# Loading the short cache in 32 KB runs, eight heads to a slot, and moving the softmax weights between the V matmuls, in a one-core decode attention kernel

## The chip, the cores and the metric

The kernel runs on one core of one Trainium2 chip. The metric is the device time of one execution in microseconds (us). Executions of one kernel agree here within about 1% (the kernel before: 248.27 to 251.29 us over 7 runs). Times quoted are medians over an experiment's runs, with the lowest and highest in brackets.

Names: PE is the matmul engine (TensorE), DVE the vector engine, ACT the scalar engine, SP the engine whose queue issues the bulk loads. SBUF is the memory that the loads fill and that `slots` and `kt` lie in, addressed here as 128 partitions; PSUM is the memory that the matmuls of this kernel write.

## The reference, cut to what matters

Two attention decode steps, A and B, of one token each, independent of each other. Both have 32 query heads on 16 key/value heads, head size 128, and a cache of 8192 positions in bf16. A looks only at the last 2048 positions, B at all of them.

```python
D, Hq, Hkv, Sk, Dh = 576, 32, 16, 8192, 128
def attend(x, k_cache, v_cache, wq, wo, W):          # A: W = 2048, B: W = 8192
    q = (x @ wq) as [32 heads, 128]
    k, v = k_cache[:, :, Sk - W:, :], v_cache[:, :, Sk - W:, :]   # each serves 2 query heads
    p = softmax(q @ k.T * Dh ** -0.5)
    return (p @ v) as [1, 4096] @ wo                 # wo: [4096, 576]
out = concatenate([A, B], axis=-1)                   # [1, 1, 1152]
```

A's K and V are 16 heads x 2048 x 128 x 2 bytes = 8.39 MB each, 16.8 MB together. B's are 67.1 MB. The four weight matrices add 18.9 MB, which gives the 102.8 MB that the profile counts.

## The kernel before, where the change touches it

The cache passes through four slots of SBUF, two for K and two for V, each of 128 partitions x 32 KB = 4 MB. There are five groups: group 0 is all of A, groups 1 to 4 are four heads of B each, two heads to a slot. In a slot of B, partition 2p+e holds 128 consecutive positions (32 KB) of head e. For A a head has only 2048 positions, so before the change a slot was filled by four loads of two heads each, and a partition held four runs of 32 positions (8 KB), one of each load:

```python
def load_kv(arrs, g, s, off, res, name):
    dst = slots[:, off:off + SLOT]                       # SLOT = 16384 bf16 = 32 KB
    def go(sp):
        if g:                                            # B
            i = 4 * (g - 1) + 2 * s
            return sp.dma_start(dst, arrs[1][0, i:i + 2, :, :].rearrange("e (p t) d -> p e (t d)", t=128))
        for m in range(4):                               # A: four loads of 1 MB
            i = 4 * m + 2 * s
            src = arrs[0][0, i:i + 2, SK - W_A:, :].rearrange("e (p t) d -> p e (t d)", t=32)
            ins = sp.dma_start(dst[:, m * UNIT:(m + 1) * UNIT], src)     # UNIT = 4096
            ...                                          # all four count on one semaphore
```

Each group then runs the same loop body: K is transposed on PE, 32 blocks of 128x128 at a time, and copied from PSUM to `kt` by ACT and DVE in turn (128x1024 each); scores; one exp; P transposed; V:

```python
def k_transpose(g, u, place):
    for q in range(4):
        ...                                              # 8 transposes into PSUM bank q
        dst = kt[:, u % NKT, q * 1024:(q + 1) * 1024]    # a plain copy, ACT for even q, DVE for odd q
def v_slot(g, s, place):                                 # 32 weights each
    for tt in range(8):
        for j in range(4):
            pe.matmul(opsum[32*j:32*j+32, s*512:(s+1)*512], lhsT=ptm[:, tt*128+32*j : ... +32],
                      rhs=v[:, :, (8*j+tt)*128 : ... +128], start=(tt == 0), stop=(tt == 7))
def v_keep(g):                                           # keep the wanted head's part, sum over the 8 parts
    diag = opsum * maskV                                 # DVE, 128x1024
    acc[:, g, :] = sum(diag)                             # DVE
```

After the last group come the final softmax weights, the output projection (`ktps`, 128 matmuls of 144 columns for A, 128 for B) and the store. The loads of `wo` go into slots that are already free:

```python
for g in range(NG):                                      # NG = 5
    ...                                                  # loads, k_transpose, k_scores, softmax_exp
    softmax_transpose(g, 18)
    if g == NG - 1:
        weights(g)                                       # before V
        combine(0, ...)
    v_slot(g, 0, 20); v_slot(g, 1, 21); v_keep(g)
wo_loads = [(0, 0, 32, ...), (1, 0, 24, ...), (1, 24, 5, ...), (1, 29, 2, ...), (1, 31, 1, ...)]  # (A or B, first column, columns)
combine(1)
...                                                      # wo_part per load, then finish_out
```

## Time and profile before

| what | value |
|---|---|
| time | 248.95 us before the change was tried; 249.53 (248.82 to 250.72, 4 runs) beside it |
| bulk load queue | 102.77 MB, 97.0% of the 16 DMA engines' time |
| PE busy | 67% of the span; DVE and ACT 35% each |
| rate of the loads while A's cache streams (26 to 62 us) | 421 GB/s |
| rate while B's streams (64 to 218 us) | 432 GB/s |

From the page of the kernel before: the DMA engines' busy share in tenths and the rate in 40 slices of the span, the bulk queue's line, and the start of the chain of work that ended last.

```profile
...
DMA  9998999999999999999999999999999999999980
GB/s 350 410 463 372 421 423 421 420 421 420 446 449 438 433 423 427 422 422 443 434 433 438 433 427 427 427 433 433 433 438 443 422 427 433 422 454 411 433 334 9
...
q1 hardware_dynamic: 5632, 102.77, 97.0%
...
PE 8%; DVE 3%; issue 1%; ACT 0%
PE opsum L540 3%; PE ktps L627 2%; PE misc L612 1%; DVE acc L384 1%; DVE diag L548 0%; DVE accs L599 0%; DVE ptm L527 0%; PE misc L518 0%; PE misc L589 0%; PE misc L577 0%; PE misc L559 0%; PE misc L578 0%; PE misc L590 0%; PE misc L560 0%;
...
```

The load stream is busy nearly everywhere and its rate hardly changes, so whatever makes the bytes arrive sooner shortens the kernel. The page's chain ends in the tail's compute. The busy table by stage of the same kernel gives the two rates that the prediction uses; the last three columns are the clock granted to PE, the DMA engines' busy share, and GB/s:

```profile
...
core 0: us, PE busy (x) PEld busy (x) DVE busy (x) ACT busy (x) POOL busy (x), PEclk, DMA share, GB/s
26.00:62.00 36.00, 27.27 (x400) 19.73 (x393) 14.20 (x24) 17.52 (x19) 0.63 (x4) 0.89 1.01 421
64.00:218.00 154.00, 112.48 (x1568) 81.25 (x1568) 63.04 (x88) 67.48 (x72) 1.88 (x12) 0.83 1.00 432
...
```

The timeline of the tail: start, duration, engine, line and operation, count, and in brackets how long the engine was idle before and what ended it.

```profile
...
237.37 3.43 PE L627 MATMUL ktps<-slots,opj 128*32 128x144 bf16 x102
...
242.01 2.18 PE L627 MATMUL ktps<-slots,opj 128*32 128x144 bf16 x127 [1.21 <-issue]
...
245.84 0.54 PE L627 MATMUL ktps<-slots,opj 128*32 128x144 bf16 x21 [1.65 <-issue]
...
246.41 0.31 DVE L633 CAST outsb<-ktps 128x144 bf16<-128x144 f32 x1 [3.55 <-PE ktps L627]
```

The output projection stops twice, 1.21 us and 1.65 us, waiting for nothing that the profile shows ("issue"). The instruction queue moved a packet of 16 KB from 239.6 to 240.7 us and one from 243.2 to 244.4 us; the stops begin at 240.8 and 244.2 us. What PE waits for in them is not shown.

### The profile page before, as it was taken

The page shows a single profiled execution, that of the slowest core. Times are in us where ns is not written, and L with a number is a line of the kernel's source. Part 1 is how long each engine was busy: PE and PEld are TensorE (multiplying, and loading weights), DVE is VectorE, ACT ScalarE, POOL GpSimd, SP SyncE. Part 2 cuts the span into 40 slices and gives each one's busy share as a digit, 9 for nine tenths or more (in the row PEclk, how much of TensorE's full clock was granted, in tenths as well). Part 3 has the DMA queues.
Part 4 walks back from the last instruction along what each step waited for, and adds up shares of the span by engine and source line. Part 5 has one row for each costly group of instructions (what it writes and reads, how often), then busy time and mean ns, then how long its engine had stood idle before and what let it go on. Part 6 is the DMA issues. An engine that isn't in the chain of part 4 may idle for free. (4 is left out here: it accounts for less than half of the span.)

```text
span 248.4 us, 5439 instructions
## 1 busy us (share of the span) xinstructions
PE 165.4 (67%) x2428; PEld 117.5 (47%) x2428; DVE 87.3 (35%) x140; ACT 87.3 (35%) x95; POOL 10.7 (4%) x48
## 2 busy tenths in 40 slices
PE   0026839992818997625999463999470999559374
PEld 0012428770408875315876223887230987335173
DVE  0001044552142555141565231656222356330500
ACT  2000027782004776102786101778100678500000
POOL 7400000000000000000000000000000000000000
PEclk9999797998595999795999775999775699955759
DMA  9998999999999999999999999999999999999980
GB/s 350 410 463 372 421 423 421 420 421 420 446 449 438 433 423 427 422 422 443 434 433 438 433 427 427 427 433 433 433 438 443 422 427 433 422 454 411 433 334 9
DMA packets 5929, 102.89 MB, mean 414 GB/s; under 512 B 928, under 2 KB 1056, under 8 KB 1312
## 3 DMA queue, kind: packets, MB, share of 16 engines
q1 hardware_dynamic: 5632, 102.77, 97.0%
q8 instruction: 6, 0.10, 0.2%
q10 hardware_dynamic: 288, 0.00, 0.1%
q14 instruction: 3, 0.02, 0.0%
HBM read 102.76 MB, written 0.00 MB: 414 GB/s over the span
## 5 line engine op out<-in xcount | busy, mean ns | idle before, releaser
L472 ACT ACTIVATE kt<-ktps 128x1024 bf16<-128x1024 bf16 x80 | 78.4, 1021 | 88.4 <-PE ktps L466 88.2
L466 PE MATMUL ktps<-ident,slots 128*128 128x128 bf16 x1280 | 87.7, 234 | 32.2 <-PEq L214 30.0
L466 PEld LDWEIGHTS ktps<-ident,slots 128*128 128x128 bf16 x1280 | 81.7, 106 | 47.6 <-issue 47.6
L475 DVE COPY kt<-ktps 128x1024 bf16<-128x1024 bf16 x80 | 55.3, 691 | 68.8 <-PE ktps L466 68.8
L540 PE MATMUL opsum<-slots,ptm 128*32 128x512 bf16 x320 | 28.7, 537 | 4.2 <-PEq L214 4.2
L487 PE MATMUL sacc<-kt,qst 128*32 128x512 bf16 x320 | 25.4, 392 | 1.9 <-PEq L214 1.9
L425 PE MATMUL opsum<-slots,xpad 128*32 128x512 bf16 x144 | 11.2, 482 | 19.0 <-DVE xpad L413 19.0
L540 PEld LDWEIGHTS opsum<-slots,ptm 128*32 128x32 bf16 x320 | 11.6, 129 | 20.0 <-issue 17.9
L425 PEld LDWEIGHTS opsum<-slots,xpad 128*32 128x32 bf16 x144 | 5.1, 117 | 24.3 <-issue 22.6
L548 DVE TENSOR_TENSOR diag<-opsum,maskV 128x1024 f32<-128x1024 f32 x5 | 6.1, 1225 | 29.3 <-PE opsum L540 29.3
L518 PE MATMUL misc<-ident,psb 128*128 128x128 bf16 x40 | 3.9, 257 | 11.6 <-PEq L214 11.6
L431 ACT ACTIVATE qrow<-opsum 128x512 bf16<-128x512 f32 x2 | 1.2, 597 | 27.3 <-PE opsum L425 27.3
L456 POOL COPY qst<-qcol 128x8 bf16<-128x8 bf16 x20 | 3.1, 191 | 162.3 <-PE sacc L487 148.2
L508 ACT ACTIVATE psb<-sacc,stat 128x1024 bf16<-128x1024 f32 x5 | 5.6, 1114 | 11.9 <-DVE stat L502 11.9
L518 PEld LDWEIGHTS misc<-ident,psb 128*128 128x128 bf16 x40 | 2.9, 114 | 14.0 <-issue 14.0
L384 DVE TENSOR_REDUCE acc<-diag 128x128 f32<-128x1024 f32 x5 | 9.4, 1871 | 0.2
L487 PEld LDWEIGHTS sacc<-kt,qst 128*32 128x32 bf16 x320 | 5.0, 94 | 7.9 <-issue 4.3
L527 DVE TENSOR_SCALAR ptm<-misc,par 128x512 bf16<-128x512 bf16 x10 | 4.4, 481 | 11.1 <-PE misc L518 11.1
L627 PE MATMUL ktps<-slots,opj 128*32 128x144 bf16 x256 | 6.4, 268 | 2.9 <-issue 2.9
L627 PEld LDWEIGHTS ktps<-slots,opj 128*32 128x32 bf16 x256 | 5.7, 118 | 3.3 <-issue 3.3
L413 DVE TENSOR_SCALAR xpad<-xtwo,par 128x5 bf16<-128x5 bf16 x4 | 0.7, 232 | 13.8 <-DMA xtwo<-in_A_x_dram 12.4
L433 DVE CAST qrow<-opsum 128x512 bf16<-128x512 f32 x2 | 1.4, 692 | 11.6 <-PE opsum L425 11.6
(60 smaller groups left out, 35.3 us busy)
## 6 DMA issues: line engine op xcount, KB each, us to landing
slots<-in_B_k_cache_dram SPq DMA_DIRECT2D x8, 4096.0 KB
slots<-in_B_v_cache_dram SPq DMA_DIRECT2D x8, 4096.0 KB
slots<-in_A_k_cache_dram SPq DMA_DIRECT2D x8, 1024.0 KB
slots<-in_A_v_cache_dram SPq DMA_DIRECT2D x8, 1024.0 KB
slots<-in_A_wq_dram SPq DMA_DIRECT2D x1, 4608.0 KB, 13.5
slots<-in_B_wq_dram SPq DMA_DIRECT2D x1, 4608.0 KB, 23.7
slots<-in_A_wo_dram SPq DMA_DIRECT2D x1, 4608.0 KB, 19.0
slots<-in_B_wo_dram SPq DMA_DIRECT2D x1, 3456.0 KB, 26.8
```

The source lines that it names most:

```text
L384: add("dve", lambda dve: dve.tensor_reduce(out, view, AX.X, ALU.add), reads=reads, writes=writes, tag=tag)
L425: ins = pe.matmul(opsum[32 * j:32 * j + 32, c * 512:(c + 1) * 512], lhsT=xpad[:, P, x, :], rhs=slots[:, o:o + 512], start=(u == 0), stop=( ...
L466: ins = pe.matmul(ktps_bf[q][:, t * 128:(t + 1) * 128], lhsT=slots[:, o:o + 128], rhs=ident[:, :], start=True, stop=True, is_transpose=True)
L472: add("act", lambda act, q=q, dst=dst: act.activation(dst, ktps_bf[q], ACT.Copy), reads=[("bank", q)], writes=[("kt", u % NKT, q)], tag="e ...
L475: add("dve", lambda dve, q=q, dst=dst: dve.tensor_copy(dst, ktps_bf[q]), reads=[("bank", q)], writes=[("kt", u % NKT, q)], tag="e%d%d" % ( ...
L487: ins = pe.matmul(sacc[32 * j:32 * j + 32, :], lhsT=qst[:, o:o + 32], rhs=rhs, start=(u == 0 and e == 0), stop=True, skip_group_check=True)
L508: return act.activation(psb[:, :].rearrange("p (x g) -> p x g", g=2), src, ACT.Exp, bias=st(C_NB + g), scale=SCALE, accum_out=st(C_L + g))
L518: ins = pe.matmul(dst[:, t * 128:(t + 1) * 128], lhsT=psb[:, t * 128:(t + 1) * 128], rhs=ident[:, :], start=True, stop=True, is_transpose= ...
L527: ins = dve.tensor_scalar(to, src, par2[:, e:e + 1], None, ALU.mult)
L540: ins = pe.matmul(opsum[32 * j:32 * j + 32, s * 512:(s + 1) * 512], lhsT=ptm[:, o:o + 32], rhs=v[:, :, b:b + 128], start=(tt == 0), stop=( ...
L548: return dve.tensor_tensor(diag[:, :, :], opsum[:, :].rearrange("p (y d) -> p y d", y=8), m, ALU.mult)
L627: ins = pe.matmul(ktps[P][32 * j:32 * j + 32, 0:OUTW], lhsT=opj[:, P, jj:jj + 32], rhs=slots[:, o:o + OUTW], start=(jj == 0), stop=(jj == ...
```

## The change

The intent was to bring A's cache in the same 32 KB runs as B's, so that its 16.8 MB would come at B's rate, and to shorten the tail. To have one run of 32 KB per partition, a slot of A must hold eight heads: partition 8p+e holds 128 positions of head e, p from 0 to 15. The score layout follows: the evictions of A's K are strided so that positions are sorted by head, exp writes every score eight times (4096 columns), P gets 32 transposes and four masked copies, and A's V becomes 64 matmuls with 128 weights instead of 64 with 32 (which took 5.30 us together in the kernel before, from 64.10 us on; one lasts 537 ns in the mean of the page, so they overlap).

In the last group, the three small steps of the softmax weights and most of the combination go between the V matmuls, and the multiply and reduce over `opsum` become eight short multiply-adds. The first projection (`q_part`) is halved in instructions too.

```diff
 def load_kv(arrs, g, s, off, res, name):
-    ...  (four loads of "e (p t) d -> p e (t d)", two heads, t=32, for A)
+    P, n, lo = (1, 2, 4 * (g - 1) + 2 * s) if g else (0, 8, 8 * s)
+    load(slots[:, off:off + SLOT],
+         lambda: arrs[P][0, lo:lo + n, (0 if P else SK - W_A):, :].rearrange("e (p t) d -> p e (t d)", t=128), ...)
 ...
 def k_transpose(g, u, place):
-            dst = kt[:, u % NKT, q * 1024:(q + 1) * 1024]
+            if g:
+                dst, src = kt[:, u % NKT, q * 1024:(q + 1) * 1024], ktps_bf[q]
+            else:
+                dst = bass.AP(tensor=kt, offset=u % NKT * UNIT + q * 256,
+                              ap=[[NKT * UNIT, 128], [2, 128], [1024, 4], [1, 2]])
+                src = ktps_bf[q].rearrange("d (x j e) -> d x j e", j=4, e=2)
 ...
+def softmax_transpose_A(g):   # 4 x (8 transposes, then a copy of 128x1024 times maskA)
+def v_slot_A(g, s):
+    for t in range(32):
+        pe.matmul(opsum[:, s*512:(s+1)*512], lhsT=kt[:, 1, t*128:(t+1)*128], rhs=v[:, :, t*128:(t+1)*128], ...)
-def v_keep(g):                # one multiply of 128x1024, one reduce
+def v_keep(g, s):             # four multiply-adds of 128x128 per slot; weights folded in for the last group
 ...
-        softmax_transpose(g, 18)
-        if g == NG - 1:
-            weights(g)
-            combine(0, (g, 18.6, LAST))
-        v_slot(g, 0, 20)
-        v_slot(g, 1, 21)
-        v_keep(g)
+        if g == 0:
+            softmax_transpose_A(g); ...; continue
+        softmax_transpose(g, 18.5)
+        if g == NG - 1: weights_top(g)
+        v_slot(g, 0, 0, 20)
+        if g == NG - 1: weights_exp(g)
+        v_slot(g, 0, 1, 20.2)
+        if g == NG - 1: weights_sum(g)
+        v_keep(g, 0)
+        v_slot(g, 1, 0, 21)
+        if g == NG - 1: combine(range(NG - 1), ...); o_columns(0)
+        v_slot(g, 1, 1, 21.5)
+        v_keep(g, 1)
```

## The prediction

> **What bounds the kernel.** The load stream. The page's queue table puts the bulk queue at 97% of 16 engines' span, 102.77 MB. Busy time by stage gives 421 GB/s while A's cache streams (26 to 62 us, 8 KB runs) and 432 GB/s while B's streams (64 to 218 us, 32 KB runs). The last bulk bytes arrive near 242.5 us of the 248.4 us span.
>
> After that a second thing binds: in the timeline the output-projection matmuls (ktps, 256 of them) stop after number 105 (240.8 to 242.0 us) and after number 232 (244.2 to 245.8 us). 127 matmuls are 254 instructions, and the instruction queue moved 16 KB at about 239.5 and 243.0 us[...]. [...]
>
> **What the change does.**
> 1. A's 16.8 MB come in 32 KB runs: at 432 instead of 421 GB/s, 1.0 us less, all on the critical path.
> 2. A's stage costs PE, ACT and DVE more: exp over 4096 instead of 1024 elements (1.1 to about 3.6 us), 32 instead of 8 transposes, four masked evictions (about 1.2 us each, as the 128x1024 TENSOR_TENSOR), and 64 V matmuls of 512 columns with 128 weights, one after the other, where four ran side by side (5.3 us then; I estimate 16 us[...]). A's V ends near 84 us instead of 69. The slots are freed later: B's first V load is issued near 77 to 79 us (67.7 before). Its turn in the queue comes near 82 us, so no hole is expected, but only 2 to 4 us are left. K of B's first group starts about 9 us later[...], and the lag is gone two groups later.
> 3. In the last group the three small matmul steps for the weights and most of the combine go between V matmuls; the multiply and reduce of V (1.23 + 1.87 us) and four scalings (0.8 us) become eight short multiply-adds, four of them after the last matmul. From V's end to the first output-projection matmul: 5.0 us before, about 2 after. V's end itself moves only 1.5 to 2 us. The projection then starts near 232.5 instead of 237.4 us and meets the weights' landing (B's main part near 239, the last part near 241.5 us)[...]. One of the two stalls should go.
>
> So the tail is load-bound again: last piece near 241.5[...], then copy and store as before (2.6 us). Span 245 to 246.
>
> **Predicted: 246.2 us, 244.0 to 249.0 in 8 of 10; faster by over 2% 0.10, within 2% 0.85, slower 0.05.**
>
> **What would show it.** Bulk rate of 26 to 62 us near 432 GB/s; no slice below 400 GB/s between 70 and 100 us; A's V matmuls ending near 84 us; one stall of the ktps matmuls instead of two; the chain ending in the projection with a wait just before.
>
> **What would make it wrong.** A hole in the load stream near 82 us[...]: plus 1 to 4 us. A's rows of eight heads, far apart in memory, loading slower than B's. [...]

Passages on how instructions are fetched and on the clock that PE would get are cut from the prediction: no run shows the first, and the second gave no measurement. Its sum was: last piece near 241.5 us, then a wait up to 242 or 243 us, then copy and store in 2.6 us; that makes 244.6 to 245.6, given as a span of 245 to 246 us and a time of 246.2 us.

## The result

The changed kernel took 288.96 us (287.84 to 289.19, 4 runs) against 249.53 us (248.82 to 250.72, 4 runs) of the kernel before. The ratio is 1.157 (95% interval 1.1505 to 1.1626): 16% slower, 39.4 us. Ratios in this document are the mean time of one kernel's runs over that of the other's of the same rounds, so they are not quite the ratio of the medians quoted. The output was correct.

The same lines of the page, after:

```profile
...
DMA  8999999999998999999999999999999999999993
GB/s 338 436 446 276 210 191 219 217 219 201 207 219 185 214 276 438 432 433 419 438 433 428 425 433 433 433 433 428 438 438 424 428 433 428 433 428 446 420 408 131
...
q1 hardware_dynamic: 3904, 102.76, 98.0%
...
DMA 9%; PE 9%; SPq 0%; DVE 0%; issue 0%
DMA slots<-in_B_wo_dram 9%; PE ktps L455 6%; PE ktps L661 1%; PE sacc L481 1%; SPq L394 0%; DVE outsb L667 0%
...
```

The queue is as busy as before (98.0%), and yet from the fourth slice to the fifteenth it moves 185 to 276 GB/s. The chain that ended last now goes through a load. The busy table by stage, with A's stretch taken as 30 to 105 us:

```profile
...
core 0: us, PE busy (x) PEld busy (x) DVE busy (x) ACT busy (x) POOL busy (x), PEclk, DMA share, GB/s
30.00:105.00 75.00, 42.78 (x424) 28.99 (x424) 27.96 (x40) 22.34 (x19) 0.73 (x4) 0.72 1.00 209
110.00:250.00 140.00, 104.76 (x1432) 74.83 (x1431) 56.45 (x100) 62.28 (x66) 2.17 (x12) 0.84 1.00 431
...
```

B's rate is what it was (431), A's has halved: 209 instead of 421 GB/s, at a busy share of 1.00. 16.78 MB take 16.78e6 / 421e9 = 39.9 us at the old rate and 80.3 us at the new one. The difference of 40.4 us accounts for the whole loss of 39.4 us; the tail gives about 1 us back (below).

The busy share hides this: it counts the time that packets take, and each packet takes longer. The packet counts show it. First the DMA view of ten microseconds of A's stretch in the kernel after, 50 to 60 us (the rate in 40 slices of 0.25 us, each packet counted where it starts, so that 131 is one packet of 32 KB; then packets, bytes and rate, then the bulk queue's packets, MB and share):

```profile
...
GB/s 0 0 0 393 524 262 131 524 262 0 0 0 0 262 655 197 131 524 262 0 131 0 131 655 262 0 262 524 131 0 0 131 0 655 393 0 262 524 131 0
DMA packets 64, 2.08 MB, mean 208 GB/s; under 512 B 0, under 2 KB 0, under 8 KB 0
...
q1 hardware_dynamic: 63, 2.06, 99.0%
...
```

And the same view of ten microseconds of B's stretch in the same run, 150 to 160 us:

```profile
...
GB/s 393 262 393 655 524 262 393 393 524 786 131 262 393 655 655 131 262 524 524 655 131 262 655 393 655 262 262 524 524 524 262 262 786 393 393 262 393 655 524 262
DMA packets 147, 4.29 MB, mean 429 GB/s; under 512 B 16, under 2 KB 16, under 8 KB 16
...
q1 hardware_dynamic: 147, 4.29, 99.7%
...
```

In A's stretch 16 engines x 10 us x 0.99 / 63 packets = 2.51 us for a packet of 32 KB. In B's it is 16 x 10 x 0.997 / 131 packets of 32 KB (4.29 MB), at most 1.22 us. The same size of packet takes twice as long. In A's stretch the packets also start in four bursts of 15 or 16, with hardly any start between them; in B's some start in every slice. This is used below.

### The profile page after: what moved, and what is told of

Read it like the earlier page. It is cut to its first block, busy times and chain, and to the rows that moved or that the text cites. A ratio compares the mean times of both kernels' runs of the same rounds, so it can differ in the third digit from the quotient of the medians.

```text
span 287.6 us, 5408 instructions
## 1 busy us (share of the span) xinstructions
PE 176.6 (61%) x2372; PEld 123.4 (43%) x2372; DVE 96.6 (34%) x180; ACT 92.0 (32%) x95; POOL 12.5 (4%) x48
## 5 line engine op out<-in xcount | busy, mean ns | idle before, releaser
L466 ACT ACTIVATE kt<-ktps 128x1024 bf16<-128x1024 bf16 x80 | 80.5, 1047 | 123.1 <-PE ktps L455 123.0
L469 DVE COPY kt<-ktps 128x1024 bf16<-128x1024 bf16 x80 | 61.9, 780 | 82.4 <-PE ktps L455 82.2
L565 PE MATMUL opsum<-slots,ptm 128*32 128x512 bf16 x256 | 23.4, 527 | 3.8 <-PEq L211 3.8
L417 PE MATMUL opsum<-slots,xpad 128*32 128x512 bf16 x72 | 7.5, 596 | 26.8 <-DVE xpad L408 26.8
L552 PE MATMUL opsum<-slots,kt 128*128 128x512 bf16 x64 | 15.8, 411 | 6.1 <-PEq L211 3.6
L417 PEld LDWEIGHTS opsum<-slots,xpad 128*32 128x32 bf16 x72 | 2.8, 137 | 30.3 <-issue 30.3
L565 PEld LDWEIGHTS opsum<-slots,ptm 128*32 128x32 bf16 x256 | 9.4, 124 | 14.8 <-issue 13.2
L582 DVE SCALAR_TENSOR_TENSOR acc<-opsum,maskV,acc 128x128 f32<-128x128 f32 x28 | 9.8, 351 | 13.7 <-PE opsum L552 9.2
L552 PEld LDWEIGHTS opsum<-slots,kt 128*128 128x128 bf16 x64 | 6.5, 104 | 15.1 <-issue 6.3
L445 POOL COPY qst<-qcol 128x32 bf16<-128x32 bf16 x20 | 3.6, 212 | 201.9 <-PE sacc L481 190.7
```

The source lines that it names most:

```text
L417: ins = pe.matmul(opsum[32 * j:32 * j + 32, P * 512:(P + 1) * 512], lhsT=xpad[:, P, u, :], rhs=slots[:, o:o + 512], start=(u == 0), stop=( ...
L445: ins = pool.tensor_copy(dst, src)
L466: add("act", lambda act, src=src, dst=dst: act.activation(dst, src, ACT.Copy), reads=[("bank", q)], writes=[("kt", u % NKT, q)], tag="e%d% ...
L469: add("dve", lambda dve, src=src, dst=dst: dve.tensor_copy(dst, src), reads=[("bank", q)], writes=[("kt", u % NKT, q)], tag="e%d%d" % (u, q))
L552: ins = pe.matmul(opsum[:, s * 512:(s + 1) * 512], lhsT=kt[:, 1, t * 128:(t + 1) * 128], rhs=v[:, :, t * 128:(t + 1) * 128], start=(t == 0 ...
L565: ins = pe.matmul(opsum[32 * j:32 * j + 32, s * 512:(s + 1) * 512], lhsT=ptm[:, o:o + 32], rhs=v[:, :, b:b + 128], start=(tt == 0), stop=( ...
```

## The experiments

All kernels below are derived from the kernel after or the kernel before, as each says. Those called wrong compute with rows in the wrong place; they load as many bytes and run the same instructions. Runs without an interval are single runs (state unknown), and are read for effects of tens of microseconds and for rates within their own trace.

The theories at the start: (M) the memory side is slow for rows of eight heads that lie 2 MiB apart, which the prediction had named as a risk. (R) The long run itself or its size is slow here. (D) The shape of the load is at fault: its outermost dimension is 16, where B's and the old one's is 64. (C) The compute of A's new stage holds the slots. The expectations call M first PITCH, then MEMORY; R "SHAPE by run length"; and D first SHAPE, then SIXTEEN.

### The old loads under the new compute

Kernel after, with A's loads put back to four of two heads each; the rest of the change stays, so the result is wrong.

```diff
-    P, n, lo = (1, 2, 4 * (g - 1) + 2 * s) if g else (0, 8, 8 * s)
-    load(..., arrs[P][0, lo:lo + n, ...].rearrange("e (p t) d -> p e (t d)", t=128), ...)
+        for m in range(4):
+            i = 4 * m + 2 * s
+            src = arrs[0][0, i:i + 2, SK - W_A:, :].rearrange("e (p t) d -> p e (t d)", t=32)
+            ins = sp.dma_start(dst[:, m * UNIT:(m + 1) * UNIT], src)
```

> The changed kernel with A's loads as before (two heads a DMA, 8 KB runs; the result is wrong on purpose, since the layout no longer fits). All theories that put the loss on A's loads expect A's cache at about 420 GB/s again and 246 to 248 us: the 1.0 us of the prediction's point 1 is given up and the rest of the prediction's gain should appear. The rival, that the added work of A's stage (exp, transposes, V with 128 weights) holds the slots and with them the stream, expects well over 250 us and holes in the stream.

Measured: 249.94 us (249.45 to 250.92, 4 runs), ratio 1.002 (0.996 to 1.008). A's rate is 422 GB/s. The whole loss is in A's loads, and theory C falls. The 246 to 248 us of the expectation were missed, though: the rest of the predicted gain did not appear. What the compute does cost can be read here too, and is taken up after the tail.

### Eight heads, 2 MiB apart or not

Kernel after, with the step from head to head made 2 MiB less 4 KiB (wrong).

```diff
-             lambda: arrs[P][0, lo:lo + n, ...].rearrange("e (p t) d -> p e (t d)", t=128)
+            return bass.AP(tensor=a.tensor, offset=...,
+                           ap=[[128 * DH, 16], [SK * DH - 2048, 8], [1, 128 * DH]])
```

> The changed kernel with one number changed: the step from head to head in A's loads is 2 MiB minus 4 KiB instead of 2 MiB (wrong result on purpose). Same rows, same 32 KB runs, same order. Theory PITCH (rows of eight heads start a multiple of 2 MiB apart and collide in memory) expects A's cache at 420 to 432 GB/s and about 246 us. Theory SHAPE (16 blocks times 8 heads of 32 KB, however placed: few large rows per engine, or blocks of 32 KB side by side) expects 210 GB/s and 288 us as now.

Measured: 289.11 us, A's rate 210 GB/s. Nothing moved (209 GB/s in the kernel after): in this kernel's loads the step of 2 MiB isn't what halves the rate.

### The same layout in runs of 8 KB

Kernel after, each load of A cut into four, each taking a quarter of every run: dimensions [16][8][4096], 8 KB runs, same final layout, correct result.

```diff
+            for m in range(4):
+                src = arrs[0][0, 8*s:8*s+8, SK - W_A:, :].rearrange("e (p m t) d -> m p e (t d)", m=4, t=32)[m]
+                ins = sp.dma_start(dst[:, m * UNIT:(m + 1) * UNIT], src)
```

> The changed kernel with each of A's loads cut into four DMAs of 8 KB runs, all eight heads in each (right result, same places in the slot). PITCH expects the rate to stay near 210 GB/s and 285 to 290 us, for the eight heads are still read side by side. SHAPE by run length (32 KB runs are the fault) expects about 420 GB/s and 247 us.

Measured: 282.95 us, A's rate 227 GB/s. Runs as short as those of the kernel before remain near half its rate, so the length isn't it (theory R). This is close to what the expectation has PITCH say, but PITCH failed in the run before this one.

### One head at a time

Kernel after, each load cut into eight, one per head: 16 rows of 32 KB that are consecutive in memory, written to every eighth partition. Correct result.

```diff
+            for e in range(8):
+                src = arrs[0][0, 8 * s + e, SK - W_A:, :].rearrange("(p t) d -> p (t d)", t=128)
+                to = bass.AP(tensor=slots, offset=e * 4 * SLOT + off, ap=[[32 * SLOT, 16], [1, SLOT]])
+                ins = sp.dma_start(to, src)
```

> The changed kernel with each of A's loads cut into eight DMAs, one per head, 16 runs of 32 KB each, to every eighth partition (right result, same bytes to the same places). If the collision comes from rows of different heads being in flight at the same moment on different engines, one head at a time removes it: 420 GB/s or more, about 246 us. If every engine already took the heads one after the other in step, this order is the same as now and the rate stays near 210 GB/s, about 288 us.

Measured: 289.02 us, A's rate 209 to 210 GB/s. Now each load reads one contiguous half megabyte, and still the rate is halved. Heads in flight side by side aren't needed for the loss. Whether their order matters is not shown: as the expectation says, the engines may have taken the heads one after the other already. What all slow loads have in common is the 16 as the outermost dimension.

### The shape alone, in the kernel before

Two kernels made from the kernel before; all else is as it was, and both are wrong. They read nearly the same contiguous megabyte in runs of 8 KB for each load of A, and they differ in how the 128 rows are written down: as 16 blocks of 8 (a step of 255 instead of 256 positions between blocks is there to keep the two dimensions from being merged), or as 128 rows.

```diff
-                src = arrs[0][0, i:i + 2, SK - W_A:, :].rearrange("e (p t) d -> p e (t d)", t=32)
+                src = bass.AP(..., ap=[[255 * DH, 16], [32 * DH, 8], [1, 32 * DH]])     # h2_outer16
+                src = bass.AP(..., ap=[[32 * DH, 128], [1, 32 * DH]])                   # h3_outer128
```

> The kernel before, its A loads changed in the source pattern alone: each 1 MB DMA reads one nearly contiguous 1 MB stretch of one head as 16 blocks of 8 rows of 8 KB (wrong result on purpose), where the kernel before reads 64 blocks of 2 rows. The source could hardly be friendlier: no rows of different heads side by side. Theory MEMORY (where the rows lie in memory is the fault, heads or block steps) expects A's cache at 420 GB/s and 249 us as before. Theory SIXTEEN (a pattern whose outermost dimension is 16[...]) expects about 210 to 228 GB/s and 281 to 289 us.

> The control to h2_outer16: the same 128 rows of 8 KB per DMA (each starts at most 4 KB away), to the same partitions in the same order, but written as one outer dimension of 128 instead of 16 blocks of 8 (wrong result on purpose). SIXTEEN expects full rate: 420 GB/s and 248 to 250 us. If reading one stretch of 1 MB is itself slow, this one is slow too: 225 GB/s and 284 us.

Measured: 284.46 us with 16 blocks, 249.71 us with 128 rows (the kernel before took 249.48, the median of 11 runs, and 248.75 beside them). The table by stage of the kernel with 16 blocks:

```profile
...
30.00:60.00 30.00, 15.85 (x208) 11.69 (x200) 7.82 (x14) 8.57 (x9) 0.00 (x0) 0.73 1.01 225
60.00:90.00 30.00, 16.08 (x208) 10.85 (x208) 7.25 (x12) 9.07 (x10) 0.63 (x4) 0.73 1.02 230
...
```

And of the kernel with 128 rows:

```profile
...
30.00:60.00 30.00, 21.74 (x316) 18.11 (x312) 12.66 (x21) 16.32 (x17) 0.32 (x2) 0.89 1.01 420
...
```

225 to 230 GB/s against 420 (last column). Memory (nearly), run length, number of loads and destination are alike. Theory D stands, and M is out for good: a friendly source is just as slow under the slow shape.

### 32 blocks of four

Kernel after, A's slots filled by two loads of four heads, runs of 16 KB, dimensions [32][4][8192] (wrong, as the compute still takes eight heads).

```diff
+            for h in range(2):
+                src = arrs[0][0, 8*s+4*h:8*s+4*h+4, SK - W_A:, :].rearrange("e (p t) d -> p e (t d)", t=64)
+                ins = sp.dma_start(dst[:, h * 2 * UNIT:(h + 1) * 2 * UNIT], src)
```

> The changed kernel with A's loads as 32 blocks times 4 heads of 16 KB runs, two DMAs a slot (wrong result on purpose: the layout no longer fits). SIXTEEN expects full rate again, 420 to 432 GB/s, and about 250 us[...]. MEMORY with heads 2 MiB apart expects something between 210 and 420 GB/s, for four heads instead of eight or two.

Measured: 248.85 us; table by stage:

```profile
...
30.00:60.00 30.00, 22.50 (x332) 16.80 (x324) 21.66 (x28) 19.19 (x18) 0.73 (x4) 0.93 0.99 416
60.00:90.00 30.00, 24.32 (x164) 14.04 (x168) 9.39 (x16) 6.65 (x6) 0.00 (x0) 0.77 1.02 436
...
```

416 and 436 GB/s: full rate with 32 blocks of four. What longer runs are worth, it leaves open. Runs of 16 KB give 416 GB/s in 30 to 60 us, where runs of 8 KB in the kernel before give 420. But that stretch holds one slow slice of the page (384 GB/s, 30.9 to 37.1 us); the four slices after it hold 424 to 429, where the kernel before has 420 or 421. This was one run, and 32 KB runs of A in a shape that keeps the rate were not tried, so the premise that longer runs stream somewhat faster is neither shown nor refuted.

### Same rows, other partitions

Kernel of the experiment "one head at a time", with one edit: the 16 rows of a head go to 16 neighbouring partitions instead of every eighth (wrong).

```diff
-                to = bass.AP(tensor=slots, offset=e * 4 * SLOT + off, ap=[[32 * SLOT, 16], [1, SLOT]])
-                ins = sp.dma_start(to, src)
+                ins = sp.dma_start(slots[16 * e:16 * e + 16, off:off + SLOT], src)
```

> As e4_by_head (one DMA per head, 16 rows of 32 KB, the same source rows in the same order), but each head's 16 rows go to 16 neighbouring partitions instead of every eighth (wrong result on purpose). MEMORY expects no change: 210 GB/s, 288 us. SIXTEEN [...] expects [...] about a quarter of full rate, 105 to 130 GB/s while A streams, and 340 to 370 us.

Measured: 345.43 us. The table by stage of "one head at a time", every eighth partition:

```profile
...
30.00:60.00 30.00, 15.24 (x188) 11.16 (x180) 11.69 (x18) 9.63 (x9) 0.00 (x0) 0.71 1.01 210
60.00:90.00 30.00, 15.63 (x180) 12.05 (x181) 9.49 (x11) 12.44 (x10) 0.72 (x4) 0.69 1.00 209
...
```

And of this kernel, neighbouring partitions:

```profile
...
30.00:60.00 30.00, 4.30 (x40) 1.60 (x40) 3.62 (x14) 0.60 (x1) 0.00 (x0) 0.50 1.03 123
60.00:90.00 30.00, 12.07 (x152) 9.64 (x152) 8.61 (x8) 8.85 (x8) 0.00 (x0) 0.67 1.00 122
...
```

The loads, their sizes and their source rows are the same; only the destination rows changed, and the rate went from 210 to 122 GB/s. The destination decides.

What the runs show is this. At the same bytes the rate follows the shape of the load, 209 to 230 GB/s with 16 as the outermost dimension and 416 to 432 with 32, 64 or 128, and it follows where the rows go, 210 GB/s with every eighth partition and 122 with 16 neighbouring ones. Why the hardware answers so is not shown. In the DMA view of the kernel after, 50 to 60 us, the packets start in four bursts of 15 or 16, each packet 2.51 us long on average; the trace shows neither which engine moved a packet nor which partitions it wrote, so the bursts don't tell either. The 105 to 130 GB/s that the expectation gave for this run were an estimate whose reason no run tests; the 122 measured lies in it.

The layout that the change wants, partition 8p+e, can't be written as one load with 32 or more blocks: the address is p times 32 KB plus e times 2 MiB, and p has only 16 values.

### The tail alone

Kernel after with everything of A put back: loads, plain evictions, P over two heads, V with 32 weights. What is left of the change is the weights between the V matmuls, the short multiply-adds and the halved first projection. Correct result.

```diff
+    (load_kv, k_transpose's eviction, softmax_exp, softmax_transpose, v_slot for g == 0 as in the kernel before)
-        if g == 0:
-            softmax_transpose_A(g)
-            for s in range(2):
-                v_slot_A(g, s)
-                v_keep(g, s)
-            continue
```

> The changed kernel with everything of A put back as in the kernel before (loads of two heads, evictions, P over two heads, V with 32 weights); left of the change are the weights between V matmuls, the short multiply-adds and the halved first projection (right result). If the rest of the prediction holds: no hole near 82 us, the tail bound by the last landing: 246.5 to 248.5 us, 0.5 to 1% faster than before. If the tail gives nothing: 249 to 250 us.

Measured: 248.36 us (248.25 to 248.58, 6 runs), ratio 0.9957 (0.9932 to 0.9982). This part is worth 1.1 us. The timeline of its tail:

```profile
...
232.87 3.63 PE L670 MATMUL ktps<-slots,opj 128*32 128x144 bf16 x122
...
236.53 0.31 DVE L676 CAST outsb<-ktps 128x144 bf16<-128x144 f32 x1 [3.25 <-PE ktps L670]
...
240.42 4.03 PE L670 MATMUL ktps<-slots,opj 128*32 128x144 bf16 x128 [3.92 <-DMA slots<-in_B_wo_dram]
244.50 0.31 DVE L676 CAST outsb<-ktps 128x144 bf16<-128x144 f32 x1 [7.66 <-PE ktps L670]
```

No stop put down to "issue" shows in the projection any more, although the instruction queue still moved two packets of 16 KB between 236 and 243 us. The projection starts at 232.66 us instead of 237.16 and A's half ends at 236.5, and then PE waits 3.92 us for one load, B's 24 columns of `wo`. B's 128 matmuls come after it in one stretch of 4.03 us at a granted clock of 0.50 (busy table of 240.4 to 244.5 us); in the kernel before 127 matmuls of the projection took 2.18 us at 1.00. The last copy is at 244.50 instead of 246.41: of the 4.5 us gained at the front, 1.9 are left at the end of this profile.

### That load in two halves

The tail alone, with one more edit: the load of 24 columns is cut into two of 12 with a semaphore each. Correct result. The tail alone was run again beside it.

```diff
-    KS = [[("k", 0)], [("k", 1, 0), ("k", 1, 1)]]
+    KS = [[("k", 0)], [("k", 1, 0), ("k", 1, 1), ("k", 1, 2)]]
-        (1, 0, 24, WQ_W, [("k", 1, 1)]),
+        (1, 0, 12, WQ_W, [("k", 1, 1)]),
+        (1, 12, 12, WQ_W + 12 * DM, [("k", 1, 2)]),
```

> t1_tail_only with B's main output-weight load (24 of 32 columns of blocks) cut into two halves with their own semaphores (right result). In t1_tail_only the 128 matmuls of B's projection stood from 236.5 to 240.4 us and then ran in 4.1 us after that one landing. If the landing is what they wait for, the first half lands near 236 us, 48 matmuls move ahead of the last landing and the end is set by the three small pieces that land last, near 243 us: 0.5 to 1.2 us less, 247.2 to 247.9 us. If the matmuls [...] at half clock take as long anyway, no change: 248.1 to 248.6 us.

> The same kernel as t1_tail_only, once more beside u1_split_wo on the same chip: 248.0 to 248.7 us.

Measured: 247.90 us (247.36 to 248.34, 6 runs) for the split, ratio 0.9938 (0.9919 to 0.9957); 248.33 (247.72 to 248.58) for the tail alone, ratio 0.9957 (0.9939 to 0.9975), against 249.43 for the kernel before. Timeline of the split:

```profile
...
232.89 3.79 PE L670 MATMUL ktps<-slots,opj 128*32 128x144 bf16 x128 [2.01 <-DMA slots<-in_A_wo_dram]
...
237.04 0.93 PE L670 MATMUL ktps<-slots,opj 128*32 128x144 bf16 x48 [0.36 <-DMA slots<-in_B_wo_dram]
...
241.18 3.09 PE L670 MATMUL ktps<-slots,opj 128*32 128x144 bf16 x80 [3.21 <-DMA slots<-in_B_wo_dram]
...
244.32 0.31 DVE L676 CAST outsb<-ktps 128x144 bf16<-128x144 f32 x1 [7.28 <-PE ktps L670]
```

48 of B's matmuls now run at 237.04 us, in the former wait, and 80 after it. But PE got the second half at 241.2 us instead of the whole at 240.4, and the rest again ran at clock 0.50. The last pieces of the chain that ended last show what sets the end now (start, duration, what):

```profile
...
224.06 18.78 DMA slots<-in_B_wo_dram
...
242.88 1.41 PE ktps L670 x29
...
```

It is the landing of the small pieces, near 243 us as the expectation said. Only about 0.4 us came of the split; the two intervals overlap, so its own gain isn't settled. It is faster than the kernel before by 0.6%, and than the kernel after by 41 us, and is the best version.

### What A's new compute costs

This needs no further run; it is the first experiment read beside the tail alone, both with the old loads. The group of K's copies on DVE in A's stage with the new compute (busy us, mean ns of one, idle before):

```profile
...
L479 DVE COPY kt<-ktps 128x1024 bf16<-128x1024 bf16 x16 | 17.9, 1186 | 12.2 <-PE ktps L465 11.6
...
```

The same group with the old compute, in the tail alone:

```profile
...
L479 DVE COPY kt<-ktps 128x1024 bf16<-128x1024 bf16 x16 | 11.1, 692 | 12.1 <-PE ktps L465 12.1
...
```

The copy with the strided destination takes 1186 ns instead of 692, for the same 128x1024 elements. But these copies did not hold up PE. In the timeline of PE the groups of score matmuls (`sacc`) come 2.45 us apart in both kernels, until PE stops. With the new compute:

```profile
...
48.28 0.64 PE L491 MATMUL sacc<-kt,qst 128*32 128x512 bf16 x8
...
50.74 0.63 PE L491 MATMUL sacc<-kt,qst 128*32 128x512 bf16 x8
...
57.32 1.13 PE L465 MATMUL ktps<-ident,slots 128*128 128x128 bf16 x9 [4.55 <-issue]
...
```

And in the kernel before:

```profile
...
48.38 0.63 PE L487 MATMUL sacc<-kt,qst 128*32 128x512 bf16 x8
...
50.83 0.63 PE L487 MATMUL sacc<-kt,qst 128*32 128x512 bf16 x8
...
57.82 0.38 PE L466 MATMUL ktps<-ident,slots 128*128 128x128 bf16 x4 [2.23 <-issue]
...
```

The stop, in which PE waits for nothing that the profile shows, is 4.55 us long instead of 2.23, and the next 32 transposes take 3.59 us where the earlier ones took 1.96. So A's scores end at 64.83 us instead of 59.72. What PE waited for in either stop is not shown. With the longer exp, the transposes and the V matmuls after that, A's V matmuls end at 89.4 us instead of 69.4, and the first V load of B is issued late, as the timeline of SP's queue shows with the new compute:

```profile
...
82.53 7.46 SPq L405 DMA_DIRECT2D slots<-in_B_v_cache_dram  x2
...
```

In the kernel before the same two loads are issued here:

```profile
...
67.72 2.27 SPq L400 DMA_DIRECT2D slots<-in_B_v_cache_dram  x2
...
```

That leaves a hole in the load stream. The table of 82 to 88 us with the new compute:

```profile
...
82.00:88.00 6.00, 6.00 (x30) 2.70 (x29) 1.40 (x4) 0.00 (x0) 0.00 (x0) 1.00 0.84 333
...
```

And in the tail alone:

```profile
...
82.00:88.00 6.00, 6.00 (x103) 4.91 (x101) 3.32 (x5) 4.88 (x6) 0.00 (x0) 1.00 1.00 431
...
```

333 GB/s against 431 for 6 us is about 0.6 MB, or 1.4 us at 431; the two times differ by 1.6 us (249.94 and 248.36, different calls; the intervals of the two ratios overlap, so the hole is the better evidence). In the kernel after this cost is hidden behind the slow loads.

## Why the prediction was wrong, point by point

**The bound was read rightly.** The load stream binds, and when its rate halved for 16.8 MB the time grew by the 40 us that the arithmetic gives.

**The step that failed is the first point: "A's 16.8 MB come in 32 KB runs: at 432 instead of 421 GB/s, 1.0 us less, all on the critical path."** The rate was 209 GB/s, and the term is +40.4 us instead of -1.0. The prediction took run length as what distinguishes the two stages (8 KB at 421, 32 KB at 432) and carried B's rate over to A. The load of A in the new shape was of another kind: 16 blocks of eight partitions instead of 64 of two. The runs show that this shape halves the rate at 8 KB (227) as at 32 KB (209), while 16 KB in a good shape keep it. Whether longer runs in a good shape would have brought the 1.0 us stays open. Where such a load's rows go was not asked; that alone moved the rate from 210 to 122 GB/s between two of the runs.

**The risk list came near and named another mechanism.** "A's rows of eight heads, far apart in memory, loading slower than B's" was the right symptom, without a size; shifting the distance by 4 KiB changed nothing, and contiguous rows were as slow. That the symptom came, for another reason than the one named, is luck. With a chance of 0.05 for slower it carried no weight.

**The costs of A's compute were mostly right where they could be seen.** Exp over 4096 elements took 3.675 us (about 3.6 said), the masked copies 1.218 us (about 1.2), the 64 V matmuls 13.99 us with the old loads and 15.8 in the kernel after (16 said). The missing term was 5.1 us at the end of K's stage, from the longer stop of PE and the slower transposes after it; the strided copies were not foreseen either, but did not hold up PE. A's V ended at 89.4 us with the old loads (84 said), B's V load was issued at 82.5 us (77 to 79 said), and the hole that was "not expected" came and cost about 1.5 us. In the kernel after A's V ended at 114.3 us.

**The tail was right at its start and mis-sized at its end.** From V's end to the projection took 1.9 us (about 2 said, 5.0 before), the projection started at 232.66 (near 232.5 said). Both stops went, where one was to stay. But the prediction had B's main part of `wo` landing near 239 us and only the last matmuls after the last landing. PE's wait for it ended at 240.4, all 128 matmuls stood behind it, and at a granted clock of 0.50 they took 4.03 us. So the tail, with the halved first projection, gave 1.1 us and not the 1.7 that the prediction's 2.7 leaves for it (248.95 - 246.2 = 2.7, less 1.0 for the loads).

**Signs named beforehand.** Bulk rate near 432 in 26 to 62 us: no, about 210 from 30 us on. No slice below 400 between 70 and 100 us: no, all of them. A's V ending near 84: no, 114.3. One stall: none. The chain ending in the projection with a wait just before: yes, a wait for the load of `wo`.

## What to carry to other kernels

Before a load is reshaped for longer runs, look at its outermost dimension and at the partitions that its rows go to: here 16 blocks of eight partitions halved the rate, with all 16 engines at work and a busy share of 1.00, while 32 of four, 64 of two and 128 kept it (416 to 432 GB/s against 209 to 230), and 16 rows to neighbouring partitions instead of every eighth took it from 210 to 122. A full DMA queue is no sign of full speed; divide busy time by packets, or read GB/s by stage, before and after. And in a tail that waits for a load, the work standing behind the landing is what counts, at the clock that it gets (here 0.50 for 4.03 us, after a wait of 3.92 us); most of the work saved in front of it only made the wait longer (4.5 us saved, 1.9 left).
